# The second chunk's tokens fetched behind V's weights, c first, the last tile in two column steps, and another written-out order of all engines

## The chip, the cores and the metric

The kernel runs on one core of a Trainium2 chip. The metric is the device time of one execution in microseconds. The core has a matmul engine (PE, with its weight loads shown as PEld), VectorE (DVE), ScalarE (ACT), GpSimd (POOL) and SyncE (SP); SP here issues nearly all DMAs, in the order in which they stand on its queue. The clock that PE was granted is 1.00 throughout.

## What is computed

One transformer block over 2048 tokens of width 448, in bfloat16. Both halves are modulated by vectors that come from `silu(c) @ w_mod`.

```python
mod = (_silu(c) @ w_mod).reshape(c.shape[0], 6, 1, -1)
sa, ca, ga, sb, cb, gb = (mod[:, i] for i in range(6))
h = _layernorm(x) * (1 + ca) + sa
x = x + ga * attention(h, wqkv, wo)     # 16 heads of 28; each query sees 8 keys, 2 apart
h = _layernorm(x) * (1 + cb) + sb
x = x + gb * (silu(h @ w1) @ w2)        # hidden width 1792
```

## The kernel before

The tokens are cut into four chunks of 512 (`NC`), each of four tiles of 128 tokens; even and odd tokens are kept apart, since a query sees only keys of its own parity. For each chunk `norm1` normalizes the tokens (`Norm`: statistics on DVE by bn_stats, L497, or on ACT by two passes, L501 and L507; the power on POOL, L513; scaling, L523 to L527), turns them so that the width lies on partitions (chunk 0 on PE, L564; the others by DMA transposes on SP, L588) and applies the modulation (`on_pe`, L571 and L573; `on_dma`, L593 and L595). `project` multiplies with the weights of q and k (L668, copied out of PSUM at L672 by ACT or DVE) and of V (L688, copied out at L681). The q and k weights are first padded to 32 columns a head (`pad`, L603 and L605): four pads, for the four pieces of the width, k 0 to 3, and the matmuls (`phases`) take the pieces in the order 0, 3, 1, 2, two matmuls at a time.

Attention works on nine key blocks of 112 tokens a parity. `logits` (L716) multiplies keys and queries of all 16 heads into four PSUM banks, ACT takes the exponential (L724), DVE multiplies with a mask (L748); `values` multiplies with V and with a column of ones (L774), DVE divides by the sums (L779, L780), and a DMA transpose on SP (L784) puts the result into `oT`. `out_proj` (L804) multiplies with wo, and DVE adds the old x (L807). wo is multiplied with its gate on DVE (L916) as soon as the modulation rows (`mod_late`, L463 to L480) are there, and two DMAs (L917, L918) then copy parts of it to other partitions. `ffn1` normalizes again, multiplies with w1 (L831) and takes silu on ACT (L839); `ffn2` multiplies with w2 (L854), DVE adds x (L859), and SP stores the tile (L862). The last tile has a function of its own, `last_tile`: it works in two column halves, of which DVE adds one (L892) and ACT copies the other (L895; x was added by a matmul with the identity, L882), and one store (L898) follows.

w1 lies in four pieces: rows for k 0, 1 and 2 in `w1`, and the last 64 rows of each half of the columns in `w13` (L388), whose DMA has a source with an outermost dimension of two. `wqk3`, the last piece of the q and k weights, is cut in the same way. FFN1's matmuls take k 0 first and then k 3, from `w13`.

What sets the order: every piece of work is an operation of a `Plan` (`P.op`), with the operations that it needs and the PSUM banks that it takes. The planner could order them by estimated times, but for the fast path the order is written out: `ORDER` (L44) lists the numbers of all operations, with a letter where DVE or ACT is chosen and the banks behind a slash. `emit` issues them in this order, so each engine's program, and SP's and ACT's DMA queues, stand in it; each engine works through its own in order and waits for semaphores. Durations given in the operations serve the planner alone. The order is thus not changed by a changed duration, only by a changed `ORDER`.

A DMA uses one of eight semaphores in turn, so a DMA also waits until the eighth before it has landed. Before the change, ACT's queue issues the second half of chunk 0's tokens and then c. SP issues the first half, two pieces of w_mod, chunk 1's tokens, wqk3, V's weights in two DMAs, the q and k weights in two, the tokens of chunks 2 and 3, and then transposes and the other weights among each other: wo, the first part of w2 and w13 follow chunk 2's transposes, the three pieces of w1 stand between the transposes of `oT`.

Of the kernel before, what the change touches and what calls it, by code (L numbers as in the profile page):

```python
# [10 lines left out]
ALU = mybir.AluOpType  # L11
# [4 lines left out]
D = 448  # L16
# [221 lines left out]
def layer(ctx, tc, io, safe):  # L238
# [635 lines left out]

    def last_tile(k, j, u):

        box, n = {}, D // 2

        def part(o, f0, f1):
            if f0 == 0:  # L880
# [13 lines left out]
        def move(o):  # L894
            S.copy(out=box["o"][:, n:D], in_=box["ps"][1][:, 0:n])  # L895
# [128 lines left out]
```

## Time and profile before

| | |
|---|---|
| runs (median; lowest to highest) | 171.99 us; 170.29 to 173.71 us, 3 runs |
| profiled execution | 170.89 us, of which the span from first to last instruction is 169.2 us |
| PE busy | 160.8 us (95%) |
| ACT, DVE, POOL busy | 116.4, 99.1, 15.5 us |
| DMA | 17.48 MB moved |

In a row of the timeline stand the start, the length until the last of the merged instructions ends (both in us from the start of the span), the engine (SPq and ACTq are the issue of a DMA), line, operation, tile written <- tiles read, partitions x elements, and the count; in brackets, how long the engine stood idle before and what ended that. A DMA row of the issues gives the size and, where it is known, the time from issue to landing. In a row of stretches stand the stretch, its length, the busy time of each engine with its number of instructions, the granted clock, the share of 16 DMA engines that was busy, and GB/s.

### The profile page before, as it was taken

The page shows a single profiled execution, that of the slowest core. Times are in us where ns is not written, and L with a number is a line of the kernel's source. Part 1 is how long each engine was busy: PE and PEld are TensorE (multiplying, and loading weights), DVE is VectorE, ACT ScalarE, POOL GpSimd, SP SyncE. Part 2 cuts the span into 40 slices and gives each one's busy share as a digit, 9 for nine tenths or more (in the row PEclk, how much of TensorE's full clock was granted, in tenths as well). Part 3 has the DMA queues.
Part 4 walks back from the last instruction along what each step waited for, and adds up shares of the span by engine and source line. Part 5 has one row for each costly group of instructions (what it writes and reads, how often), then busy time and mean ns, then how long its engine had stood idle before and what let it go on. Part 6 is the DMA issues. An engine that isn't in the chain of part 4 may idle for free.

```text
span 169.2 us, 4278 instructions
## 1 busy us (share of the span) xinstructions
PE 160.8 (95%) x1763; PEld 79.9 (47%) x1764; DVE 99.1 (59%) x259; ACT 116.4 (69%) x166; POOL 15.5 (9%) x38
## 2 busy tenths in 40 slices
PE   7878999999999999999999999999999999999990
PEld 2344444353465554554464454564444454444670
DVE  2788899999988859475476309972950405100120
ACT  3676999899779967879996989484429903248000
POOL 4313112010000410011000000021001100000000
PEclk9999999999999999999999999999999999999999
DMA  5994999859994453500614001226410061100022
GB/s 180 251 324 171 190 303 164 265 154 101 142 248 109 112 103 76 169 0 9 119 27 111 2 0 31 54 63 117 113 54 6 0 124 38 49 0 0 27 62 68
DMA packets 32312, 17.48 MB, mean 103 GB/s; under 512 B 24157, under 2 KB 31453, under 8 KB 32285
## 3 DMA queue, kind: packets, MB, share of 16 engines
q1 hardware_dynamic: 32132, 16.90, 42.9%
q8 instruction: 16, 0.26, 0.7%
q10 hardware_dynamic: 152, 0.23, 0.4%
q14 instruction: 12, 0.09, 0.2%
HBM read 9.12 MB, written 1.84 MB: 65 GB/s over the span
## 4 chain that ended last, share of the span: by engine, by line
PE 74%; DMA 9%; DVE 7%; ACT 5%; issue 2%; SPq 0%
PE psum L831 25%; PE psum L854 24%; PE psum L804 7%; PE psum L668 6%; DMA wqk<-in_A_wqkv_dram 5%; PE psum L688 4%; PE psum L774 4%; PE psum L716 2%; DMA x_all<-in_A_x_dram 2%; DMA oT<-o 2%; DVE p L748 2%; PE psum L885 2%; ACT both L501 1%; ACT wp L603 1%; DVE wqk L595 1%
## 5 line engine op out<-in xcount | busy, mean ns | idle before, releaser
L831 PE MATMUL psum<-h,w 64*128 64x512 bf16 x392 | 43.7, 376 | 0.0
L854 PE MATMUL psum<-w,both 128*128 128x448 bf16 x210 | 42.1, 353 | 0.0
L839 ACT ACTIVATE both<-psum 128x1024 bf16<-128x1024 f32 x28 | 27.3, 1021 | 13.6 <-PE psum L831 13.6
L724 ACT ACTIVATE p<-psum 128x896 bf16<-128x896 f32 (+1 forms) x36 | 31.7, 935 | 5.0 <-PE psum L716 4.7
L831 PEld LDWEIGHTS <-w 64*128 64x128 bf16 x392 | 19.3, 94 | 22.2 <-issue 0.7
L854 PEld LDWEIGHTS <-both 128*128 128x128 bf16 x210 | 19.6, 98 | 19.1 <-issue 1.6
L513 POOL TENSOR_TENSOR rs<-rs,negh 128x2 f32<-128x2 f32 x16 | 12.5, 778 | 118.0 <-DVE rs L510 82.6
L748 DVE TENSOR_TENSOR p<-p,maskb 128x1792 bf16<-128x1792 bf16 (+1 forms) x18 | 19.5, 1099 | 4.8 <-ACT p L724 4.8
L859 DVE TENSOR_TENSOR ot<-psum,x_all 128x448 bf16<-128x448 f32 x15 | 9.2, 618 | 20.2 <-PE psum L854 15.9
L668 PE MATMUL psum<-h,wp 64*128 64x512 bf16 x168 | 19.8, 377 | 0.5 <-ACT wp L603 0.4
L668 PEld LDWEIGHTS <-wp 64*128 64x128 bf16 x224 | 10.4, 94 | 12.8 <-ACT wp L603 0.9
L507 ACT ACTIVATE mrow<-x_all,mv 128x448 bf16<-128x448 bf16 x16 | 10.7, 668 | 3.4 <-DVE mv L504 3.0
L804 PE MATMUL psum<-wo,oT 64*128 64x448 bf16 x112 | 12.7, 350 | 0.1
L593 ACT ACTIVATE h<-h,modc 128x512 bf16<-128x512 bf16 x7 | 5.5, 806 | 10.2 <-DMA h<-xn 10.2
L672 ACT CAST qk<-psum 128x1024 bf16<-128x1024 f32 x12 | 12.0, 1018 | 0.6 <-PE psum L668 0.6
L688 PE MATMUL psum<-wv,h 64*128 64x448 bf16 x98 | 11.3, 350 | 1.2 <-DMA wv<-in_A_wqkv_dram 1.1
L807 DVE SCALAR_TENSOR_TENSOR x_all<-psum,x_all 128x448 bf16<-128x448 f32 x16 | 9.5, 619 | 3.6 <-PE psum L804 3.6
L780 DVE TENSOR_TENSOR o<-psum,rc 112x448 bf16<-112x448 f32 (+1 forms) x18 | 11.2, 624 | 0.6
L779 DVE RECIPROCAL rc<-psum 112x16 f32<-112x16 f32 (+1 forms) x18 | 4.5, 251 | 10.2 <-PE psum L774 9.5
L774 PEld LDWEIGHTS <-p 128*128 128x128 bf16 x288 | 8.2, 96 | 3.3 <-issue 1.7
L774 PE MATMUL psum<-v,p 128*128 128x29 bf16 x288 | 9.0, 176 | 0.0
L595 DVE TENSOR_SCALAR h<-h,modc 128x512 bf16<-128x512 bf16 x17 | 6.1, 406 | 4.8 <-DMA h<-xn 4.6
(95 smaller groups left out, 144.6 us busy)
## 6 DMA issues: line engine op xcount, KB each, us to landing
out_dram<-ot SPq DMA_DIRECT2D x16, 112.0 KB, 1.8
both<-in_w_mod_dram SPq DMA_DIRECT2D x1, 1568.0 KB, 8.4
x_all<-in_A_x_dram SPq DMA_DIRECT2D x3, 448.0 KB, 8.1
w<-in_B_w_dram SPq DMA_DIRECT2D x3, 448.0 KB
w<-in_B_w_dram SPq DMA_DIRECT2D x1, 896.0 KB, 7.0
both<-in_w_mod_dram SPq DMA_DIRECT2D x2, 392.0 KB, 5.7
w<-in_B_w_dram SPq DMA_DIRECT2D x1, 672.0 KB, 5.4
wv<-in_A_wqkv_dram SPq DMA_DIRECT2D x2, 224.0 KB, 8.5
```

What stands on the lines that cost most here:

```text
L513: G.tensor_tensor(out=rs[:, j:j + n], in0=rs[:, j:j + n], in1=negh[:, 0:n], op=ALU.pow)
L668: return T.matmul(ps[:, j, :], lhsT=w.rearrange("p h d -> p (h d)"), rhs=h[rows, :, t, 128:128 + CP], start=start, stop=stop)
L672: copy_on(o)(out=qk[:, :, g, :, s0:s0 + CP], in_=ps.rearrange("p j (t s) -> p j t s", t=2))
L688: T.matmul(ps[:, par, 0:D], lhsT=h[rows, par, t, b0:b0 + 128], rhs=wv[rows, t, :], start=start, stop=stop)
L724: S.activation(out=out_, in_=ps[:, :, 0:4 * nq].rearrange("p j (g q) -> p j g q", q=nq), func=ACTF.Exp, scale=SCALE)
L748: V.tensor_tensor(out=p, in0=p, in1=maskb[:, 1 if b == 0 else 0, 0:nq].unsqueeze(1).to_broadcast([128, H, nq]), op=ALU.mult)
L774: T.matmul(ps[:, h, 0:DH + 1], lhsT=p[:, at:at + 128], rhs=v[:, h, 0:DH + 1], start=True, stop=True)
L780: V.tensor_tensor(out=box["o"][0:nq, off:off + D].rearrange("p (h d) -> p h d", d=DH), in0=ps[0:nq, :, 0:DH], in1=r.unsqueeze(2).to_broadc ...
L804: T.matmul(ps[par][:, 0:D], lhsT=oT[rows, t, par, s0:s0 + 128], rhs=wo[rows, par, t, :], start=start, stop=stop)
L831: return T.matmul(ps[:, j, :], lhsT=w, rhs=h[rows, :, t, :], start=start, stop=stop)
L839: silus[k].append(P.op(("act", 904.0), lambda o, i=i, box=box: S.activation(out=hid[:, k % 2, :, i, :], in_=box["ps"], func=ACTF.Silu), [m ...
L854: T.matmul(box["ps"][:, 0:D], lhsT=hid[:, k % 2, f % 2, f // 2, 128 * j:128 * j + 128], rhs=w2[:, f // 2 + 7 * (f % 2), :], start=(f == 0) ...
```

## The change

Four edits come together. First, c is loaded ahead of the tokens on ACT's queue. Second, the tokens of chunk 1 (448 KB) are made to depend on the issue of V's weights, and stand behind them on SP's queue, ahead of wqk3; those of chunks 2 and 3 come as one DMA of 896 KB in place of two. Third, the last tile is done in two column steps: its first 224 columns with all 14 matmuls, an add and a store of their own, ahead of two whole tiles; at the very end the other 224 columns in two pieces of 112, of which DVE adds one and ACT copies the other, and a second store. Fourth, `ORDER` is another, so that the order of the instructions on all engines differs, and with it which of ACT and DVE does a copy. Among what moves on SP's queue is w13: it now stands behind the two transposes of FFN chunk 0's input, as the last load ahead of FFN1; the first part of w2 stands ahead of wo; and the first transpose into `oT` stands ahead of the two copies of wo (L917 and L918; in the changed kernel lines from here on are some lines further down). The lag of 300 to 230 is an estimate for the planner.

```diff
@@ -42,29 +42,29 @@
 
 
 ORDER = (
-    "1 60/0 46 47 6 0 4 7 5 80 81 8 2 9 61 63 66 88 3 69 89 70/2 62 10 22 16 48 90 67 18 19 82 55 20 87 91 71 73/2 83 84 21 11 85v 74 97/3/4 86v 98 64 92 "
...
+    "1 44 45 46 47 0 4 5 52 7 8 78 9 58/0 2 59 6 3 67 68/2 69 60 62 79 80 71/2 10 11 51 86 87 88 63 65 85 89 20 18 72 22 23 56 81 90 16 82 57 83v 84v 92 "
...
 )
 
 
@@ -365,10 +365,10 @@
 
     def first_x(i):
         return dict(out=x_all[:, 2 * i:2 * i + 2, :].rearrange("p t d -> p (t d)"), in_=x_view[0, :, i, :])
-    act_q = [P.op(("none", 0.0), lambda o: nc.scalar.dma_start(**first_x(1)))]
-    act_q.append(P.op(("none", 0.0), lambda o: nc.scalar.dma_start(out=c4[:], in_=c.rearrange("o (k p) -> (o k) p", p=KM)), act_q[-1:]))
-    ld_c = [P.op(("none", 5200.0), lambda o: S.preload_act_table(ACTF.Silu), act_q[-1:])]
-    ld_x = [[load(224, **first_x(0)), P.op(("none", 4400.0), none, act_q[:1])]]
+    act_q = [P.op(("none", 0.0), lambda o: nc.scalar.dma_start(out=c4[:], in_=c.rearrange("o (k p) -> (o k) p", p=KM)))]
+    act_q.append(P.op(("none", 0.0), lambda o: nc.scalar.dma_start(**first_x(1)), act_q[-1:]))
+    ld_c = [P.op(("none", 3900.0), lambda o: S.preload_act_table(ACTF.Silu), act_q[-1:])]
+    ld_x = [[load(224, **first_x(0)), P.op(("none", 4800.0), none, act_q[-1:])]]
 
     def load_mod(k0, k1, c0, c1, after=()):
         return load((c1 - c0) * (k1 - k0) * KM / 512, wmod[0:KM, k0:k1, c0:c1], w_mod[KM * k0:KM * k1, c0:c1].rearrange("(k p) n -> p k n", p=KM), after)
@@ -380,7 +380,8 @@
     b = load(224, wqk[:, 1, :].rearrange("p (a n) -> p a n", a=2), dram(A_wqkv, 128, 0, ((1, 0, 128), (64, D, 2), (0, 1, D))), late)
     ld_qk = [[a], [b], [a], [load(112, wqk3[:], dram(A_wqkv, 128, D, ((128, -D, 2), (1, 0, K3), (0, 1, D))), late)]]
     ld_v = [load(224, wv[:, 2 * a:2 * a + 2, :], dram(A_wqkv, 192 * a, 2 * D, ((1, 0, 128), (128, 0, 2), (0, 1, D))), late) for a in range(2)]
-    ld_x += [[load(448, x_all[:, 4 * k:4 * k + 4, :].rearrange("p (i t) d -> p i (t d)", t=2), x_view[k], late)] * 2 for k in range(1, NC)]
+    ld_x.append([load(448, x_all[:, 4:8, :].rearrange("p (i t) d -> p i (t d)", t=2), x_view[1], [x["deps"][0] for x in ld_v])] * 2)
+    ld_x += [[load(896, x_all[:, 8:16, :].rearrange("p (k i t) d -> p k i (t d)", i=2, t=2), x_view[2:4].rearrange("c p i n -> p c i n"), late)] * 2] * 2
     ld_m2 = [load_mod(0, 4, 2 * D, 6 * D, late)]
     ld_o = [load(336, wo[:, 0, 0:3, :], rows3(A_wo), late), load(56, wo[half(0), 0, 3, :], A_wo[384:D, :], late)]
     ld_1 = [load(448, w1[:, k, :], B_w1[r:r + 128, :], late, rate=0.3) for k, r in ((0, 0), (2, 320))]
@@ -632,7 +633,7 @@
                 for part in range(2):
                     mm(box["ps"], part, kk, False, kk == 2, part)
         a = P.op(("pe", 4 * step), straight, deps, take=("one", "one") if split else ("big",), mode=1)
-        return box, a, P.op(("pe", 3 * step), crossed, [a], mode=1, lag=300.0)
+        return box, a, P.op(("pe", 3 * step), crossed, [a], mode=1, lag=230.0)
 
     qk_done, v_of, v_take, v_op, qk_mm, v_mm, halo = {}, {}, {}, {}, {}, {}, {}
     h1_done, h1_part = {}, {}
@@ -874,38 +875,43 @@
 
     def last_tile(k, j, u):
 
-        box, n = {}, D // 2
-
-        def part(o, f0, f1):
+        box, cut = {}, (0, D // 2, 3 * D // 4, D)
+
+        def part(o, f0, f1, i0, i1):
             if f0 == 0:
-                box["ps"] = [onet(), onet()]
-                T.matmul(box["ps"][1][:, 0:n], lhsT=ident[:], rhs=x_all[:, u, n:D], start=True, stop=False)
+                box.setdefault("ps", []).extend(onet() for _ in range(i0, i1))
+                if i1 == 3:
+                    T.matmul(box["ps"][2][:, 0:cut[3] - cut[2]], lhsT=ident[:], rhs=x_all[:, u, cut[2]:cut[3]], start=True, stop=False)
             for f in range(f0, f1):
-                for i in range(2):
-                    T.matmul(box["ps"][i][:, 0:n], lhsT=hid[:, k % 2, f % 2, f // 2, 128 * j:128 * j + 128], rhs=w2[:, f // 2 + 7 * (f % 2), n * i:n * i + n],
-                             start=(f + i == 0), stop=(f == NF - 1))
+                for i in range(i0, i1):
+                    T.matmul(box["ps"][i][:, 0:cut[i + 1] - cut[i]], lhsT=hid[:, k % 2, f % 2, f // 2, 128 * j:128 * j + 128], rhs=w2[:, f // 2 + 7 * (f % 2), cut[i]:cut[i + 1]],
+                             start=(f == 0 and i < 2), stop=(f == NF - 1))
 
         def hold(o):
             box["o"] = outb[o["slot"]["out"]]
 
-        def add(o):
-            V.tensor_tensor(out=box["o"][:, 0:n], in0=box["ps"][0][:, 0:n], in1=x_all[:, u, 0:n], op=ALU.add)
+        def add(o, i):
+            V.tensor_tensor(out=box["o"][:, cut[i]:cut[i + 1]], in0=box["ps"][i][:, 0:cut[i + 1] - cut[i]], in1=x_all[:, u, cut[i]:cut[i + 1]], op=ALU.add)
 
         def move(o):
-            S.copy(out=box["o"][:, n:D], in_=box["ps"][1][:, 0:n])
-
-        def store(o):
-            nc.sync.dma_start(out=out_view[u // 4, u // 2 % 2, u % 2], in_=box["o"][:])
-        prev = None
-        for f0, f1 in ((0, 4), (4, 8), (8, 12), (12, 14)):
-            need = silus[k][f0 // 2:f1 // 2] + w2_gated + ([x1_done[u]] if f0 == 0 else [])
-            prev = P.op(("pe", 194.0 * (f1 - f0) + (98.0 if f0 == 0 else 0.0)), lambda o, f0=f0, f1=f1: part(o, f0, f1), need + [prev], take=("one", "one") if f0 == 0 else ())
-            if f0 == 0:
-                first = prev
-        ot = P.op(("none", 0.0), hold, [first], take=("out",))
-        ad = P.op(("dve", 310.0), add, [prev, ot], give=((first, "one"),))
-        mv = P.op(("act", 242.0), move, [prev, ot], give=((first, "one"),))
-        sp(550.0, store, [ad, mv], 1200.0, ((ot, "out"),), (390.0, 500.0, 360.0))
+            S.copy(out=box["o"][:, cut[2]:cut[3]], in_=box["ps"][2][:, 0:cut[3] - cut[2]])
+
+        def store(o, i, n):
+            nc.sync.dma_start(out=out_view[u // 4, u // 2 % 2, u % 2][:, cut[i]:cut[n]], in_=box["o"][:, cut[i]:cut[n]])
+        prev, done = None, []
+        for i0, i1 in ((0, 1), (1, 3)):
+            for f0, f1 in ((0, 8), (8, 14)):
+                need = silus[k][f0 // 2:f1 // 2] + w2_gated + ([x1_done[u]] if f0 == 0 else [])
+                prev = P.op(("pe", 97.0 * (f1 - f0) + (50.0 if i0 and not f0 else 0.0)), lambda o, a=(f0, f1, i0, i1): part(o, *a), need + [prev], take=("one",) * (i1 - i0) if f0 == 0 else ())
+                if f0 == 0:
+                    first = prev
+            if i0 == 0:
+                ot = P.op(("none", 0.0), hold, [first], take=("out",))
+                done = [P.op(("dve", 310.0), lambda o: add(o, 0), [prev, ot], give=((first, "one"),))]
+                sp(550.0, lambda o: store(o, 0, 1), done, dma=(390.0, 500.0, 250.0))
+            else:
+                ad = [P.op(("dve", 195.0), lambda o: add(o, 1), [prev, ot], give=((first, "one"),)), P.op(("act", 150.0), move, [prev, ot], give=((first, "one"),))]
+                sp(550.0, lambda o: store(o, 1, 3), ad, 1200.0, ((ot, "out"),), (390.0, 500.0, 250.0))
 
 
     for k in range(NC):
```

44 rows, old and new, of the table ORDER are left out of this document.

## The prediction, made before the changed kernel was run

> **What bounds the kernel now.** I read the busy shares and slices first, then a table of stretches, then the timeline of each stretch, then the DMA issues.
>
> ```profile
> PE 160.8 (95%) x1763; PEld 79.9 (47%) x1764; DVE 99.1 (59%) x259; ACT 116.4 (69%) x166; POOL 15.5 (9%) x38
> PE   7878999999999999999999999999999999999990
> PE 74%; DMA 9%; DVE 7%; ACT 5%; issue 2%; SPq 0%
> ```
> ```profile
> 16.00:44.00 28.00, 27.50 (x382) 12.33 (x380) 26.90 (x59) 26.79 (x42) 3.23 (x7) 1.00 0.85 194
> 44.00:66.00 22.00, 22.00 (x336) 11.83 (x334) 17.42 (x46) 17.86 (x26) 2.62 (x2) 1.00 0.67 126
> 66.00:122.00 56.00, 56.00 (x634) 28.46 (x630) 33.53 (x81) 43.87 (x58) 2.76 (x4) 1.00 0.28 64
> 122.00:165.00 43.00, 43.00 (x325) 21.67 (x324) 10.17 (x30) 18.04 (x25) 1.38 (x2) 1.00 0.14 35
> ```
> The columns of the second fence are the stretch, its length, then busy time of PE, PEld, DVE, ACT, POOL, the granted clock, DMA share and GB/s. From 44 to 165 us PE is never idle, so nothing can be won there, and whatever makes PE wait there is paid in full. From 16 to 44 us PE, DVE and ACT are all near full; PE idles 0.50 us. Before 16 us the start waits for loads. The change keeps PE's work, so a gain has to come from the start or from the tail.
>
> **The start (V's weights ahead of the second chunk's tokens, c first).**
>
> ```profile
> 12.16 3.27 PE L688 MATMUL psum<-wv,h 64*128 64x448 bf16 x28 [1.05 <-DMA wv<-in_A_wqkv_dram]
> 14.03 1.78 ACT L603 COPY wp<-wqk 128x896 bf16<-128x896 bf16 x2 [1.29 <-DMA wqk<-in_A_wqkv_dram]
> 14.73 0.39 DVE L603 COPY wp<-wqk 128x896 bf16<-128x896 bf16 x1 [0.79 <-DMA wqk<-in_A_wqkv_dram]
> 15.80 2.72 SPq L588 DMA_TRANSPOSE h<-xn  x2
> 15.86 7.97 PE L668 MATMUL psum<-h,wp 64*128 64x512 bf16 x70 [0.43 <-ACT wp L603]
> 21.43 0.80 ACT L593 ACTIVATE h<-h,modc 128x512 bf16<-128x512 bf16 x1
> 22.14 1.90 ACT L672 CAST qk<-psum 128x1024 bf16<-128x1024 f32 x2
> 23.76 0.73 PE L716 MATMUL psum<-qk 28*128 28x128 bf16 x16
> ```
> V's matmuls waited 1.05 us for wv; with wv ahead of 560 KB (x of chunk 1 and wqk3) this wait goes. What is late next is wqk: the bytes ahead of it on SP's queue are the same set in another order, so it lands at 14.03 again. The pads now are k 0 and 1 on ACT and k 2 and 3 on DVE (before: 2 and 0 on ACT, 1 and 3 on DVE), so the first q/k matmul (k 0) can start after one ACT pad, at 14.03+0.89=14.9 instead of 15.86. But its third pair needs pad k 1 at 15.8, and the next bound is ACT: from 14.03 to chunk 1's h at 21.43 it runs the same ten instructions in both orders (two pads, two V copies, four sums, two squares). Chunk 1's h therefore comes at 21.4 to 22.2 again, PE waits there instead, and the early start is given back: 0. Chunk 1's tokens land later by V's 448 KB, some 1.2 us at the 378 GB/s of the row of 13 us below. DVE's statistics of them move behind it; the old order held DVE until 14.73 for a pad, so its transposes, at 15.80 before, move by about 0.2 us, under ACT's chain. Moving c saves nothing: the modulation weights decide the first h. One DMA for chunks 2 and 3 carries the same bytes, and their first reader (ACT's sums) stands behind the V copies: 0.
>
> **The order from 22 to 44 us.** The first logits wait for three q/k copies; the new order has these three on ACT behind h (22.14+3x0.95=25.0) where the old one shared them with DVE. So L716, at 23.76 before, moves by 1.2 us, and PE does 8 more L668 matmuls meanwhile (0.86 us): +0.35. Further on:
>
> ```profile
> 29.31 0.94 PE L463 MATMUL psum<-both,screp 112*32 112x448 bf16 x16
> 33.99 1.08 DVE L916 TENSOR_TENSOR wo<-wo,gbc 128x1792 bf16<-128x1792 bf16 x1
> 35.10 0.54 SPq L917 DMA_DIRECT2D wo<-wo  x1
> 41.94 1.39 PE L804 MATMUL psum<-wo,oT 64*128 64x448 bf16 x8
> ```
> ```profile
> wo<-wo SPq DMA_DIRECT2D x1, 168.0 KB, 5.7
> ```
> ```profile
> 39.34 3.02 DMA oT<-o
> 54.64 0.76 PE psum L804 x8
> ```
> The last fence is from the chain of work that ended last: start, length, what. The modulation rows (L463) move behind 56 matmuls of L668, 28 of L688, three L716 and one L774, where 42, 14, two and none preceded them from chunk 1's start. That is some 3.5 us, so the wo gate on DVE (35.07 before) ends near 38 and the two shifted copies of wo start 3 us later. SP now issues the first oT transpose ahead of them, the second behind. The first L804 took 1.39 us where eight such matmuls take 0.76, a wait of 0.6 that ends with oT (39.34+3.02=42.36). I followed the new queues of PE, ACT and DVE with these durations up to it: it ends near 44.2 (before: 43.3) with 8 more L668 matmuls done (0.86). Sum of the stage: 0. Bounds: the gain can be no more than PE's 0.50 idle, the 0.6 and the two start waits (1.05+0.43), 2.6 us in all; the loss is some 1.5 us if the wo copies take 5.7 us again behind a gate at 38 and PE waits for them.
>
> **The step that decides: w13 on SP's queue.** The last piece of B_w1 (w13, 224 KB, L388) stood in row 28.50 below as the second DMA. In the new order it stands behind both transposes of FFN chunk 0's h and is the last load ahead of FFN1.
>
> ```profile
> w<-in_B_w_dram SPq DMA_DIRECT2D x1, 224.0 KB
> ```
> ```profile
> 13.00:14.00 1.00, 1.00 (x14) 0.62 (x12) 0.91 (x5) 0.00 (x0) 0.71 (x2) 1.00 1.06 378
> 35.20:36.00 0.80, 0.80 (x11) 0.26 (x8) 0.80 (x4) 0.80 (x2) 0.24 (x1) 1.00 0.14 52
> ```
> ```profile
> 28.50 2.34 SPq L362 DMA_DIRECT2D w<-in_B_w_dram  x2
> 58.66 3.98 SPq L588 DMA_TRANSPOSE h<-xn  x2
> 64.54 0.81 ACT L593 ACTIVATE h<-h,modc 128x512 bf16<-128x512 bf16 x1 [1.74 <-DMA h<-xn]
> 64.61 1.05 DVE L595 TENSOR_SCALAR h<-h,modc 128x512 bf16<-128x512 bf16 x3
> 65.16 0.73 PE L804 MATMUL psum<-wo,oT 64*128 64x448 bf16 x6
> 65.73 3.40 PE L831 MATMUL psum<-h,w 64*128 64x512 bf16 x30
> ```
> ```profile
> x_all<-in_A_x_dram SPq DMA_DIRECT2D x1, 224.0 KB, 3.3
> ```
> At 35.2 us w13 alone is under way: DMA share 0.14, that is 2 of 16 engines, and 52 GB/s, against 378 GB/s with all engines. Its source has an outermost dimension of two, so two engines carry it. Its 229 KB need 229/52=4.4 us on the wire. In the old order it was issued by 30.84 and FFN1 began at 65.73, so all of this was hidden. Now: SP was free after the second h transpose at 62.64. PE's work ahead of the first L831 is the same in both orders, but the out projection that feeds this transpose stands ahead of one L716 and two L774 now (0.31+0.8 us), so I take 61.9 for w13's issue. The first two x loads of the same size, issued together, took 3.3 us to land, of which 458 KB at 378 GB/s are 1.2 us of data; so I take 2.1 us for lead and completion. It lands at 61.9+2.1+4.4=68.4; without the earlier transpose at 69.1. PE reaches the first FFN1 matmul at 65.7, does the pair of k 0 (0.2), and the next pair is k 3, which reads w13: it waits from 65.95 to 68.4 or 69.1. I take the first, 2.4 us. Everything else of PE stands behind it in order. Bounds: 0.5 (PE itself a microsecond late, w13 issued earlier still) and 3.5.
>
> The Trainium skill, page "DMA: Bandwidth & Descriptors", section "Why a DMA increments its semaphore by 16 and not by 1", has the number of engines as the largest number up to 16 that divides the slowest dimension, and so two here, as the share of 0.14 has it. By that page's 27 GiB/s for an engine ("Specifications") the data would take an estimated 4.0 us and the stall would be 0.4 us shorter than mine; the measured 52 GB/s decides.
>
> **The last tile.**
>
> ```profile
> 62.28 0.96 PE L774 MATMUL psum<-v,p 128*128 128x29 bf16 x32
> ...
> 164.25 0.62 DVE L859 TENSOR_TENSOR ot<-psum,x_all 128x448 bf16<-128x448 f32 x1 [2.29 <-DMA out_dram<-ot]
> 165.10 0.39 DVE L892 TENSOR_TENSOR ot<-psum,x_all 128x224 bf16<-128x224 f32 x1 [0.23 <-PE psum L885]
> 165.14 0.35 ACT L895 CAST ot<-psum 128x224 bf16<-128x224 f32 x1 [9.00 <-PE psum L885]
> 165.55 0.33 SPq L898 DMA_DIRECT2D out_dram<-ot  x1
> ```
> 14 of the 28 matmuls of 224 columns become 28 of 112: the same columns, and 32 matmuls of 29 columns, each with a weight load of its own, in 0.96 us (row 62.28) show that weight loads keep up. The last add goes from 0.39 to about 0.27 us (0.62 for 448 columns, 0.39 for 224). The three last whole tiles now share one output buffer: tile 13's add waits for tile 12's store, as the 2.29 us above do now, and the first half's add stands behind it on DVE. Gain 0.1, bounds -0.3 and +0.5; the last store's landing stays.
>
> **Sum.** 170.89 (profiled execution, span 169.2) + 0 (start) + 0 (22 to 44 us) + 2.4 (w13) - 0.1 (tail) = 173.2. The median of the runs is 171.99, 1.1 above the profiled execution, which would make 174.3; I predict 173.8, between the two, and add the same 0.6 to the profiled basis in each rival.
>
> **Rivals.** First: w13 arrives in time: 170.89-0.1+0.6=171.4, to 171.9 with a rest of the stall. For it speaks that PE or h could be late themselves; against it that w13's issue and h hang on the same transpose: h needs its landing and a modulation (64.54+0.81-62.64=2.7 us after SP is free), w13 needs 2.1+4.4=6.5. It decides when PE comes to FFN1 after 68. Second, faster: PE's start gain is kept because chunk 1's h comes earlier, the stage to 44 us loses its waits, and w13 is none. At most 2.6+0.1, so 168.8 to 170.5; it needs ACT's chain to be shorter than its 7.4 us, and the new order has none of its instructions gone. Third, slower still: the wo copies behind the late gate hold PE at the first L804 by 1.5 us, and w13 by 2.4: 170.89+3.9-0.1+0.6=175.3; it decides when the gate ends after 38. Fourth, PE's clock:
>
> ```profile
> 1.26 4.88 PE L416 MATMUL psum<-both 128*128 128x512 bf16 x11 [1.26 <-DVE both L313]
> 6.92 1.04 PE L416 MATMUL psum<-both 128*128 128x512 bf16 x4
> ```
> The first matmuls took 4.88/11=0.44 us each, later ones 0.26. If the wait at 66 us returned PE to that pace for 4.88 us, this would cost 4.88x(1-0.26/0.44)=2.0 us more: 175.8. The wait of 1.05 us before V left no such slow matmuls. The Trainium skill, page "TensorE: Matmul & The Clock Gate", Part 1, halves the clock after an idle window of about 3.4 us; no wait in this trace is that long.
>
> **How the numbers follow.** w13's stall as computed 0.57, w13 in time 0.20, faster 0.08, wo and w13 0.10, clock 0.05. The likeliest's own range is 171.5 to 175.5 (stall 0.5 to 3.5, basis up to 0.6 either way). The range 170.2 to 176.2 leaves out the lower part of the faster case and the tail of the last two. Two per cent (3.4 us, about what a measurement of this kernel tells from no change) is 168.55 below and 175.43 above: above lie the last two cases and the upper edge of the first, 0.20; below only the second rival's far end with the scatter of the runs, 0.04; within 0.76.
>
> **What would show it.** After: V without a wait for wv near 11 us; the first L669 near 15; chunk 1's h still at 21.4 to 22.2; and in the waits of PE one L832 of about 2.4 us near 66 us that ends with the DMA of B_w. Wrong would be: no PE gap near 66 us, w13 on 16 engines, or a PE gap of a microsecond between 22 and 44.

## The result and the profile after

| | before | after |
|---|---|---|
| median of the runs | 171.25 us (170.29 to 173.71, 6 runs) | 178.24 us (176.91 to 178.56, 6 runs) |
| profiled execution, span | 169.2 us | 176.4 us |
| mean granted clock of it | 1.00 | 0.984 |

The changed kernel is slower: ratio 1.041, 95% interval 1.035 to 1.046, or 7 us. The forecast was 173.8 us with a range of 170.2 to 176.2; the time lies 2.0 us above the range.

The page of the changed kernel, PE's busy slices and the granted clock (a slice is 4.4 us):

```profile
PE   7987999999989992999999999999999999999990
PEclk9999999999999999699999999999999999999997
PE 66%; DMA 12%; ACT 7%; DVE 6%; issue 2%; SPq 2%; POOL 2%; ACTq 0%; DVEq 0%
```

PE has one hole, in the slice from 66 us on, and the next slice has a granted clock of 0.6. Before, neither was there. In the chain of work that ended last, PE has 66% and DMA 12%, where PE had 74% and DMA 9%.

The same stretches in numbers (columns as in the prediction's table):

```profile
16.00:44.00 28.00, 26.86 (x362) 12.38 (x359) 24.32 (x57) 27.00 (x42) 4.85 (x5) 1.00 0.80 193
44.00:66.00 22.00, 21.16 (x336) 11.48 (x337) 19.24 (x47) 17.59 (x26) 1.69 (x2) 1.00 0.57 113
66.00:71.00 5.00, 1.23 (x14) 0.44 (x12) 3.44 (x9) 3.51 (x6) 0.00 (x0) 1.00 1.40 81
71.00:76.00 5.00, 5.00 (x34) 1.95 (x32) 0.00 (x0) 1.33 (x2) 0.00 (x0) 0.66 0.50 142
76.00:127.00 51.00, 51.00 (x583) 26.56 (x581) 31.82 (x76) 35.36 (x45) 2.85 (x4) 1.00 0.25 54
```

From 44 to 66 us PE idles 0.84 us where it never idled before; from 66 to 71 it works 1.23 us out of 5; from 71 to 76 it is busy throughout, at a clock of 0.66. From 76 us on it is never idle again up to its last matmul, which ends at 171.9 us, ahead of the last slice with its clock of 0.7. Cut finer, the stretch shows that 0.6 and 0.66 are means of two values:

```profile
71.72:75.12 3.40, 3.40 (x18) 1.23 (x16) 0.00 (x0) 0.55 (x1) 0.00 (x0) 0.50 0.49 149
75.13:78.50 3.37, 3.37 (x36) 1.64 (x34) 0.09 (x1) 1.77 (x3) 0.00 (x0) 1.00 0.02 5
```

For 3.4 us the clock stands at half, and then it is full again. PE's timeline says what each of these is (start, length, what, and in brackets the idle time before it and what ended that):

```profile
10.75 3.30 PE L689 MATMUL psum<-wv,h 64*128 64x448 bf16 x28
14.70 0.60 PE L669 MATMUL psum<-h,wp 64*128 64x512 bf16 x4 [0.65 <-ACT wp L604]
...
21.66 3.00 PE L669 MATMUL psum<-h,wp 64*128 64x512 bf16 x22 [0.33 <-DVE h L596]
24.84 0.40 PE L717 MATMUL psum<-qk 28*128 28x128 bf16 x16 [0.18 <-ACT qk L673]
...
44.29 0.38 PE L717 MATMUL psum<-qk 28*128 28x112 bf16 x16 [0.42 <-DVE qk L673]
51.20 1.04 PE L669 MATMUL psum<-h,wp 64*128 64x512 bf16 x8 [0.55 <-ACT v L682]
...
66.72 0.38 PE L832 MATMUL psum<-h,w 64*128 64x512 bf16 x2
70.87 4.88 PE L832 MATMUL psum<-h,w 64*128 64x512 bf16 x28 [3.77 <-DMA w<-in_B_w_dram]
75.59 0.92 PE L805 MATMUL psum<-wo,oT 64*128 64x448 bf16 x8
```

FFN1 (L832 here, L831 before) does its first pair at 66.72 and then waits 3.77 us for w13. SP's timeline and the chain of work show the load that it waits for:

```profile
61.30 1.54 SPq L589 DMA_TRANSPOSE h<-xn  x1
62.90 0.61 SPq L362 DMA_DIRECT2D w<-in_B_w_dram  x1
64.82 2.52 SPq L785 DMA_TRANSPOSE oT<-o  x2
```
```profile
62.90 7.92 DMA w<-in_B_w_dram
```

The load is issued at 62.90 and lands 7.92 us later. Two stretches of that time (last two columns: DMA share, GB/s):

```profile
64.50:65.00 0.50, 0.50 (x10) 0.26 (x6) 0.47 (x3) 0.22 (x1) 0.00 (x0) 1.00 0.00 0
68.00:70.00 2.00, 0.00 (x0) 0.00 (x0) 1.86 (x5) 1.51 (x4) 0.00 (x0) 1.00 0.13 50
```

From 64.5 to 65.0 us, 1.6 us after the issue, nothing moves; from 68 to 70 us 0.13 of 16 engines, that is two, move 50 GB/s.

With these lines the 7.2 us between the two spans can be laid out along PE's work. FFN1 starts at 66.72 where it started at 65.73: 1.0. The wait: 3.8. Its first 30 matmuls took 3.40 us before, so 28 of them 3.40x28/30 = 3.2; they take 4.88 now: 1.7. That makes 6.5 by 75.6 us; the remaining 0.7 lies behind that. The last add is at 171.92, where it was at 165.10, so 0.3 came up to there and 0.4 after it:

```profile
171.92 0.28 DVE L894 TENSOR_TENSOR ot<-psum,x_all 128x112 bf16<-128x112 f32 x1 [0.45 <-PE psum L887]
```

SP's two last issues, the stores of the first half and of the second:

```profile
171.62 0.38 SPq L900 DMA_DIRECT2D out_dram<-ot  x1
...
172.26 1.55 SPq L900 DMA_DIRECT2D out_dram<-ot  x1
```

Before, the last store's issue took 0.33 us (165.55).

### The profile page after: what moved, and what is told of

Its sections match the earlier page's. It is cut to its first block, busy times and chain, and to the rows that moved or that the text cites. A ratio compares the mean times of both kernels' runs of the same rounds, so it can differ in the third digit from the quotient of the medians.

```text
span 176.4 us, 4308 instructions
## 1 busy us (share of the span) xinstructions
PE 163.4 (93%) x1778; PEld 81.0 (46%) x1778; DVE 100.3 (57%) x261; ACT 115.5 (65%) x164; POOL 16.8 (10%) x38
## 4 chain that ended last, share of the span: by engine, by line
PE 66%; DMA 12%; ACT 7%; DVE 6%; issue 2%; SPq 2%; POOL 2%; ACTq 0%; DVEq 0%
PE psum L832 25%; PE psum L855 23%; DMA wqk<-in_A_wqkv_dram 5%; PE psum L805 5%; DMA w<-in_B_w_dram 4%; PE psum L669 4%; PE psum L717 3%; PE psum L689 2%; DMA h<-xn 2%; PE psum L775 2%; POOL rs L514 2%; SPq L362 2%; ACT qk L673 2%; PE psum L887 2%; ACT both L502 1%
## 5 line engine op out<-in xcount | busy, mean ns | idle before, releaser
L832 PE MATMUL psum<-h,w 64*128 64x512 bf16 x392 | 45.7, 387 | 3.8 <-DMA w<-in_B_w_dram 3.8
L832 PEld LDWEIGHTS <-w 64*128 64x128 bf16 x392 | 20.1, 96 | 26.9 <-DMA w<-in_B_w_dram 4.2
L514 POOL TENSOR_TENSOR rs<-rs,negh 128x2 f32<-128x2 f32 x16 | 13.7, 859 | 125.3 <-DVE rs L511 125.3
L669 PE MATMUL psum<-h,wp 64*128 64x512 bf16 x168 | 20.9, 377 | 1.8 <-ACT wp L604 0.9
L673 ACT CAST qk<-psum 128x1024 bf16<-128x1024 f32 x13 | 12.9, 1019 | 1.0 <-PE psum L669 1.0
L805 PE MATMUL psum<-wo,oT 64*128 64x448 bf16 x112 | 12.8, 350 | 0.0
L594 ACT ACTIVATE h<-h,modc 128x512 bf16<-128x512 bf16 x6 | 4.8, 808 | 11.0 <-DMA h<-xn 11.0
L511 DVE TENSOR_SCALAR rs<-mv 128x2 f32<-128x2 f32 x16 | 2.6, 163 | 12.6 <-ACT mrow L508 12.5
L775 PE MATMUL psum<-v,p 128*128 128x29 bf16 x288 | 9.5, 176 | 0.0
```

The source lines that it names most:

```text
L514: G.tensor_tensor(out=rs[:, j:j + n], in0=rs[:, j:j + n], in1=negh[:, 0:n], op=ALU.pow)
L669: return T.matmul(ps[:, j, :], lhsT=w.rearrange("p h d -> p (h d)"), rhs=h[rows, :, t, 128:128 + CP], start=start, stop=stop)
L673: copy_on(o)(out=qk[:, :, g, :, s0:s0 + CP], in_=ps.rearrange("p j (t s) -> p j t s", t=2))
L775: T.matmul(ps[:, h, 0:DH + 1], lhsT=p[:, at:at + 128], rhs=v[:, h, 0:DH + 1], start=True, stop=True)
L805: T.matmul(ps[par][:, 0:D], lhsT=oT[rows, t, par, s0:s0 + 128], rhs=wo[rows, par, t, :], start=start, stop=stop)
L832: return T.matmul(ps[:, j, :], lhsT=w, rhs=h[rows, :, t, :], start=start, stop=stop)
```

## The experiments

Theory A: w13 stands too late on a queue that gives it two engines, PE waits for it, the wait lowers PE's clock, and that is nearly all of the loss. Rival B: the new order costs the time as a whole, and w13's wait merely covers other waits. A number by which a kernel "gains" is taken against 178.24, which was measured at another time than the runs; ratios are against the kernel before on the same chip, beside the run, where its median was 171.1 to 171.8 us. Each load has a second number in `ORDER`, for its landing, which issues nothing and moves with it; the cuts show it in run 2 alone.

**1. w13 early (changed kernel).** Only the load's token (its number in `ORDER`) moves, to the place that it had among the weight loads.

```diff
-... 230 231 34 279/6 280 ... 350 366 38 359/0 ...
+... 230 231 34 38 279/6 280 ... 350 366 359/0 ...
```

> The changed kernel, with one load moved: w13 (224 KB of B_w1) is issued among the other weight loads of the middle stage, ahead of the second transpose of chunk 0's h, as the kernel before does it. Nothing else differs. Theory A (w13 on two engines, issued too late, and TensorE's clock after the wait, are nearly all of the loss): the wait of 3.8 us at the first L832 goes, the 28 matmuls behind it take 3.2 us and not 4.9, and the time falls from 178.2 by 5.5 to 6 us to 172.2 to 172.8, about 1 us above the kernel before. Rival B (the new order as a whole costs the time, and w13's wait only covers other waits, that of h above all): the wait at FFN1 stays in part under another name, and the time stays at 175 or more. If the start of the new order were worth something after all, the time would fall below 171.

Measured: 174.09 us, ratio 1.015 (1.009 to 1.021). The clock stays full and FFN1 has no wait, a gain of 4.2 us. But 2.6 us of loss are left, more than theory A's 1: FFN1 begins only at 68.50, since PE now waits at an out projection (L804 here).

```profile
55.71 1.04 PE L804 MATMUL psum<-wo,oT 64*128 64x448 bf16 x8 [1.67 <-DMA oT<-o]
68.50 3.40 PE L831 MATMUL psum<-h,w 64*128 64x512 bf16 x30
```

Both theories hold in part: A has the larger share, but B has one.

**2. w13 late (kernel before).** The converse: the load's token behind both transposes of FFN chunk 0's h, all else as before.

```diff
-... 42 234v 43 40 210v ... 368 396 397 395 ...
+... 42 234v 43 210v ... 368 396 40 397 41 395 ...
```

> The kernel before, with w13's load alone moved behind both transposes of FFN chunk 0's h. Theory A: PE waits at the first FFN1 group (65.73 us before). SP is free after the second transpose at 62.64; a landing 8.0 us after the issue, as in the changed kernel (62.90 to 70.87), puts the end of the wait at 70.6: 4.6 us of wait, and 1.8 us more for the slow clock behind it, so 171.3 + 6.4 = 177.5 to 178. Rival B: with the old order around it the wait is mostly covered, 172 to 174. Rival C (the wait costs, but the clock does not fall in this order): 175.5 to 176.

Measured: 177.94 us, ratio 1.038 (1.031 to 1.044). This one token makes the kernel before as slow as the changed kernel.

```profile
PEclk9999999999999998599999999999999999999997
```
```profile
65.42 0.38 PE L830 MATMUL psum<-h,w 64*128 64x512 bf16 x2
71.16 5.58 PE L830 MATMUL psum<-h,w 64*128 64x512 bf16 x28 [5.36 <-DMA w<-in_B_w_dram]
```

(L830 here.) PE comes to FFN1 1.3 us earlier than in the changed kernel, so it waits longer, 5.36 us, and the 28 matmuls take 5.58. Rivals B and C both fall: in the old order nothing covers the wait, and the clock drops there too.

**3. w13 in two DMAs (changed kernel).** Place unchanged; two DMAs of 64 rows each.

```diff
-ld_1.append(load(224, w13[:], dram(B_w1, 128, F // 2, ((128, -F // 2, 2), (1, 0, K3), (0, 1, F // 2))), late, rate=0.3))
+def two(o):
+    for a, (r, c0) in enumerate(((128, F // 2), (256, 0))):
+        nc.sync.dma_start(out=w13[half(a), :], in_=B_w1[r:r + K3, c0:c0 + F // 2])
+ld_1.append(sp(max(400.0, 224 / 0.31), two, [begin] + late, 500.0, dma=(600.0, 1300.0, 150.0 + 224 / 0.3))[0])
```

> The changed kernel, with w13's load left at its place but cut into two transfers of 64 rows each, whose outermost dimension is 64 and not two. Theory A (two engines at 52 GB/s carry it): with 16 engines the 224 KB need 0.6 to 1.2 us on the wire in place of 4.4, so w13 lands some 3.2 to 3.8 us earlier, at 67.1 to 67.7; the wait falls to 0.2 to 0.9 us, the clock stays, and the time is 172.4 to 173.8. Rival D (not the wire but the queue delays it: the issue at 62.90 itself, lead and completion, or the transposes ahead of it): the wait stays at 3 us or more and the time at 177 or more.

Measured: 174.03 us, ratio 1.018 (1.010 to 1.026).

```profile
w<-in_B_w_dram SPq DMA_DIRECT2D x2, 112.0 KB, 2.7
```
```profile
66.61 3.52 PE L835 MATMUL psum<-h,w 64*128 64x512 bf16 x30
```

The two halves land 2.7 us after their issue instead of 7.9 and FFN1 has no wait, at the same place in the queue: rival D falls. The rule in the Trainium skill, page "DMA: Bandwidth & Descriptors", section "Why a DMA increments its semaphore by 16 and not by 1" (the largest number up to 16 that divides the slowest dimension), gives 16 engines for 64 rows and two for the old source. The traces agree: 0.13 of 16 engines for the old source, and for the halves a landing after 2.7 us, though their engines were not counted.

**4, 5 and 9. The wait filled with matmuls (changed kernel).** 17 matmuls of 512 columns on landed data, into a PSUM tile that the group behind them starts anew. Runs 4 and 5 differ from 9 in the group alone: `(k, i)` was (0, 0) and (0, 1), and the one that stands first in PE's order is (0, 4).

```diff
+            for _ in range(fill):
+                T.matmul(box["ps"][:, 0, :], lhsT=ident[:], rhs=w1[:, 0, 0:512], start=True, stop=True)
             for kk in (0, 3, 1, 2):
...
-            box, first, m = phases(mm(i), 512, nrm.done + ld_1)
+            box, first, m = phases(mm(i), 512, nrm.done + ld_1, fill=17 if (k, i) == (0, 4) else 0)
```

> The changed kernel, with 17 matmuls of 512 columns put ahead of the first FFN1 group, on data that landed long before, into a PSUM tile that the group then starts anew (their result is overwritten). They need 17 x 0.213 = 3.6 us at full clock and lie inside the wait of 3.8 us. Theory A (the clock falls because PE is idle for 3.8 us): the granted clock stays full, the 28 matmuls behind the wait take 3.2 us and not 4.9, and the time falls by 1.5 to 2 us to 176.2 to 176.8, though the wait for w13 still ends at 70.9. Rival E (the slow matmuls are slow for another reason, such as operands or transfers at that place): they stay at 4.9 us and the time at 178 or above.

> The changed kernel with the 17 filling matmuls of 512 columns ahead of the FFN1 group that comes first in PE's order (in the run before they had been put ahead of a group that comes ten microseconds later). They lie inside the wait for w13, 66.7 to 70.9. Theory A (PE's idle time of 3.8 us lowers the clock): no slice of the granted clock below 9, the 28 matmuls behind the wait take 3.2 to 3.4 us and not 4.9, time 178.2 - 1.7 = 176.2 to 176.8, with the wait for w13 still ending at 70.9. Rival E (they are slow for another reason): 4.9 us again, and the time at 178 or above.

> The changed kernel with the 17 filling matmuls now at their place, ahead of the FFN1 group that stands first in PE's order (the two runs before had them behind it, at 81 us). They run while w13 is awaited. Theory A (PE's idle time of 3.8 us lowers the clock): no slice of the granted clock below 9, the 28 matmuls behind the wait take 3.2 to 3.4 us and not 4.9, the wait for w13 still ends at 70.9 to 71.1, and the time is 178.2 - 1.7 = 176.2 to 176.8. Rival E (they are slow for another reason than idle time): 4.9 us again and the time at 178 or above.

Measured: run 4 183.4 us (1.066, 1.055 to 1.077), run 5 183.07 us (1.067, 1.061 to 1.073), run 9 176.32 us (1.029, 1.023 to 1.034). Runs 4 and 5 missed their purpose: the matmuls came behind the wait and only made the kernel longer, as the first fence shows. Run 4 tells only that 17 of them are 3.84 us, and, in the second fence, that the matmuls behind a wait of 4.14 us are slow again.

```profile
81.95 3.84 PE L622 MATMUL psum<-w,ident 128*128 128x512 bf16 x17
```
```profile
71.22 5.80 PE L834 MATMUL psum<-h,w 64*128 64x512 bf16 x28 [4.14 <-DMA w<-in_B_w_dram]
```

Run 9 has them in the wait:

```profile
PEclk9999999999999999999999999999999999999999
```
```profile
67.74 3.84 PE L622 MATMUL psum<-w,ident 128*128 128x512 bf16 x17
71.51 3.41 PE L834 MATMUL psum<-h,w 64*128 64x512 bf16 x30
```

Here the granted clock stays full, 30 matmuls take 3.41 us as in the kernel before, and the time is 1.9 us lower (2.1 by the two ratios), although w13 lands no earlier. So the slow matmuls come from PE's idle time and rival E falls. What a drop costs hangs on how long the clock stays down. First run 2, then run 4:

```profile
69.20:76.00 6.80, 4.84 (x24) 1.82 (x26) 1.14 (x2) 0.35 (x1) 0.00 (x0) 0.50 0.47 126
69.72:76.53 6.81, 5.31 (x26) 1.90 (x28) 0.15 (x1) 2.38 (x4) 0.00 (x0) 0.50 0.45 123
```

In these two the clock stood at half for 6.8 us, and PE worked 4.84 and 5.31 us of them; in the changed kernel it was 3.4 us, all of them worked. Half of each is 2.4, 2.7 and 1.7 us, and by 2.4, 2.6 and 1.7 us the 28 matmuls were longer than 3.2 (5.58, 5.80 and 4.88). So the loss doesn't follow the order of the waits, which were 5.36, 4.14 and 3.77 us.

The Trainium skill, page "TensorE: Matmul & The Clock Gate", Part 1, has the clock halved after an idle window of about 3.4 us, with windows that run free of the kernel's start. The traces agree in part: the stretches at half clock are one or two times 3.4 us long, they come with the waits of 3.77, 4.14 and 5.36 us, and the wait of 1.67 us (run 1) left the clock at 1.00. But in the changed kernel PE still worked 0.83 of the 3.40 us ahead of the drop (68.30 to 71.70), and in the profiled execution of run 7, below, the clock fell at the kernel's start with no such wait:

```profile
5.60:9.00 3.40, 2.39 (x41) 1.49 (x40) 2.08 (x11) 1.70 (x5) 2.15 (x9) 1.00 1.08 303
9.02:12.42 3.40, 3.40 (x24) 2.00 (x22) 2.19 (x7) 2.74 (x6) 0.12 (x1) 0.50 1.08 319
```

Ahead of that drop PE worked 2.39 of 3.40 us, and its longest wait there was 0.74 us. In the kernel before it worked 2.16 of the 3.40 us from 9.00 to 12.40, and the clock stayed full. What brings the drop in run 7 is not found. The clock of 1.00 in the kernel before, too, is that of its profiled execution: of its 23 runs beside runs 9 to 12, six had a mean clock of 0.989 or 0.990, which is what one such stretch would make, and took 171.9 to 173.2 us; the others had 0.995 or more and a median of 170.7.

**6. One last store (kernel of run 3).** The last tile's row is stored once, behind both column steps.

```diff
-                sp(550.0, lambda o: store(o, 0, 1), done, dma=(390.0, 500.0, 250.0))
+                sp(550.0, none, done, dma=(390.0, 500.0, 250.0))
...
-                sp(550.0, lambda o: store(o, 1, 3), ad, 1200.0, ((ot, "out"),), (390.0, 500.0, 250.0))
+                sp(550.0, lambda o: store(o, 0, 3), ad, 1200.0, ((ot, "out"),), (390.0, 500.0, 250.0))
```

> The kernel with w13 in two DMAs, and the last tile's row stored by one DMA behind both of its column steps, in place of one DMA for each step. In the kernel with two stores SP took 0.38 us to issue the first half's and 1.51 us to issue the second, where a store takes 0.33 us elsewhere, so that SP ended 1.2 us later than it would. Theory T (the second store's issue is held up by the stores right ahead of it): with one store the last issue takes 0.3 to 0.4 us and the time falls by 0.8 to 1.2 us, from 174.0 to 172.8 to 173.2. Rival U (the last store is slow wherever it stands, or the end of the program waits for something else): 173.7 or more.

Measured: 174.13 us, ratio 1.017 (1.013 to 1.021), against 174.03 for run 3: by the runs no difference. In the profile the last issue does take 0.33 us, at 167.03, and the span is 171.2 in place of 171.8; but runs of this order scatter by 2 us (172.71 to 174.74) for a reason that run 10 looks for. The issue is shown, its worth in time is not, by this run.

**7. The start of the change alone (kernel before).** V's loads ahead of the second chunk's tokens, k 0's pad first on ACT. c stays behind the tokens, and the tokens of chunks 2 and 3 stay two DMAs.

```diff
-... 10 22 16 48 90 67 18 19 82 55 20 ... 13 78a 68 79v 76a ...
+... 10 18 20 22 16 48 90 67 19 82 55 ... 13 76a 68 79v 78a ...
```

> The kernel before with the start of the change alone: V's two loads ahead of the second chunk's tokens, and the first of ACT's two pads is that of k 0. All the rest of the order is the old one. The prediction's step (the early start is given back, since ACT's chain sets chunk 1's h): V's matmuls lose their wait of 1.05 us, the first q/k matmul comes at 14.7 to 15.0, chunk 1's h at 21.2 to 22.2 as before, PE waits for it, and the time is that of before within 0.4 us. Rival S (the start is worth something in itself, and the new order behind it loses it): 0.7 to 1.3 us faster than before. Rival R (the later tokens delay chunk 1's h): 0.5 us or more slower.

Measured: 171.37 us, ratio 1.002 (0.999 to 1.004): no difference. The wait for wv is gone, q/k starts 0.7 us earlier, and PE loses it again at chunk 1's h. (V itself starts no earlier here, at 12.35 where it was 12.16, since this execution has the half clock from 9.02 to 12.42 us. The other 11 runs have a mean clock of 0.995 or more and took 170.9 to 172.2 us.)

```profile
12.35 3.02 PE L687 MATMUL psum<-wv,h 64*128 64x448 bf16 x28
15.18 6.22 PE L667 MATMUL psum<-h,wp 64*128 64x512 bf16 x56
21.95 2.03 PE L667 MATMUL psum<-h,wp 64*128 64x512 bf16 x14 [0.55 <-DVE h L594]
23.91 0.63 PE L715 MATMUL psum<-qk 28*128 28x128 bf16 x16
```

The first logits come at 23.91, where they came at 23.76. Rivals S and R fall; the prediction's step holds as far as this run has it, without c.

**8 and 12. Chunk 1's h ahead of work for later chunks.** Run 8 is run 6's kernel, run 12 is run 7's.

```diff
 run 8
-... 70 183 235 191 193 192 182 110 184 185 234 108v ... 194 161a ...
+... 70 183 235 191 193 192 110 108v ... 194 161a 234 182 184 185 ...
 run 12, beside run 7's
-... 119a 77v 114/0 147v 105/1 26 148v ... 195 194 196 109 110v 115 164a ...
+... 119a 147v 148v 77v 114/0 105/1 26 ... 109 110v 115 164a 195 194 196 ...
```

> The kernel with w13 in two DMAs and one last store, and chunk 1's h modulated ahead of work for later chunks: one sum of ACT's (0.77 us) and one pair of DVE statistics (0.8 us) move behind it. In the changed kernel h's second transpose had landed at 19.9 while ACT came to h at 21.26 and DVE at 20.56. If ACT's and DVE's order, and not the transfer, holds h: h ends at 20.9 to 21.1 on both, PE's wait of 0.33 us for it goes, and the time is 0.3 to 0.5 us below that of the kernel with one last store. If the lead of 0.75 us that PE has there is lost further on anyhow (v and q/k copies of 44 to 51 us): no difference.

> An attempt at a version that beats both kernels: the kernel before with V's loads ahead of the second chunk's tokens and k 0's pad first (0.2% from before in its run), and now with what chunk 1's h waits for moved up: DVE makes the first two xn tiles ahead of its second pad, and two of ACT's sums for later chunks (0.77 us each) stand behind h. In the run without these moves PE waited 0.55 us for h, whose transpose landed at 21.1 by DVE's wait. If that wait was all that ate the early start: 0.4 to 0.7 us faster than before (170.4 to 170.8). If the copies of q and k, which follow h on ACT and DVE, are next: no difference within 0.3 us.

Measured: run 8 173.75 us, ratio 1.014 (1.009 to 1.019); run 12 171.03 us, ratio 0.998 (0.995 to 1.002). PE's wait for chunk 1's h is gone in both, and waits for other copies stand in its place. In run 8:

```profile
15.96 8.41 PE L671 MATMUL psum<-h,wp 64*128 64x512 bf16 x74 [0.23 <-ACT wp L606]
25.10 0.40 PE L719 MATMUL psum<-qk 28*128 28x128 bf16 x16 [0.73 <-ACT qk L675]
```

Where the changed kernel waits 0.33 us for h and then 0.18 for a q/k copy, this one waits 0.73 for the copy. Its median is 0.4 us below run 6's, which would fit the first of the two expectations, but the two intervals overlap, so neither is shown. In run 12 PE waits 0.41 and 0.2 us for copies of q and k instead. Run 12 was to beat both kernels; it can't be told from the kernel before, and no other run is faster.

**10. The load behind the fourth oT transpose (kernel of run 6).** The load of k 1 (448 KB) moves among the early weights.

```diff
-... 231 34 279/6 ... 380 381 36 355/2/1 ...
+... 231 34 36 279/6 ... 380 381 355/2/1 ...
```

> The kernel with w13 in two DMAs and one last store, and the load of k 1 of B_w1 (448 KB) issued some 23 us earlier, with the other weights, so that it no longer stands right behind the fourth oT transpose at 52 us. In two of the profiled executions of kernels of this order PE waited 1.5 to 1.7 us for that transpose at 55.7: the last piece of it landed at 55.6, behind that load's first data, where it landed at 53.1 in the others. Theory L (the load delays the transpose's last piece): no wait of over 0.3 us at the L804 of 54 to 56 us, and the time falls from 174.1 by 0.8 to 1.5 us. Rival M (the wait comes from the transposes' own issue, 1.3 us longer in those executions): the wait stays in some executions and the time within 0.4 us of 174.1.

Measured: 173.62 us, ratio 1.014 (1.010 to 1.019), 0.5 us below run 6, with intervals that overlap. The wait at the out projection is still there, at 55.19, now with ACT's v copy put down as what ended it:

```profile
55.19 1.04 PE L807 MATMUL psum<-wo,oT 64*128 64x448 bf16 x8 [1.35 <-ACT v L684]
```

Theory L falls. What goes with the wait is the row of M, SP's issue of one transpose of h at 44 to 45 us. First run 10, then run 6, whose profiled execution had no such wait:

```profile
44.66 2.44 SPq L591 DMA_TRANSPOSE h<-xn  x1
47.15 5.18 SPq L787 DMA_TRANSPOSE oT<-o  x4
```
```profile
44.87 1.23 SPq L592 DMA_TRANSPOSE h<-xn  x1
46.15 5.76 SPq L788 DMA_TRANSPOSE oT<-o  x4
```

In runs 1, 5, 8, 9 and 10 this issue took 2.1 to 2.5 us and PE waited 1.35 to 1.67 us at 55 us; in the changed kernel and in runs 3, 4 and 6 it took 1.23 us and there was no such wait. That is all that is shown; what makes the issue long in some executions wasn't found.

**11. The last tile of the change alone (kernel before).** The new last tile's function, and its tokens at the places of the old one's.

```diff
-... 751/2/3 729 ... 661 755 662 752 733 734 735 753 754 757 756 758 759 704 ...
+... 751/2 729 ... 661 662 752 733 734 735 757/3/1 753 754 755 756 758 760 759 761 762 704 ...
```

> The kernel before with the last tile of the change alone: two column steps, two stores, three accumulators. The prediction had -0.1 us for it (bounds -0.3 to +0.5). Theory T (the last store's issue takes 1.5 us right behind the store of the first half, and nothing is won in the arithmetic): 0.6 to 1.1 us slower than before. If the prediction's -0.1 holds: the same within 0.3 us.

Measured: 172.09 us, ratio 1.005 (1.002 to 1.009), that is 0.9 us slower (0.3 to 1.5). Its last add ends at 165.96 and SP has 0.99 us of issue left:

```profile
165.68 0.28 DVE L893 TENSOR_TENSOR ot<-psum,x_all 128x112 bf16<-128x112 f32 x1 [0.46 <-PE psum L886]
```
```profile
166.02 0.99 SPq L899 DMA_DIRECT2D out_dram<-ot  x1
```

The add is shorter by 0.1 us, as forecast, the last issue is longer by 0.7 us. Theory T holds for the time; the issue itself took 0.99 us and not 1.5.

## Why the prediction was wrong

- **The start (0): right.** V without a wait at 10.75, first q/k at 14.70 (forecast 14.9), ACT's h from 21.26 (forecast 21.4 to 22.2), first logits 1.1 us later (forecast 1.2). Run 7 has the start without the move of c at +0.3 us (0.2%), which is not clear of zero. c by itself was not tried.
- **22 to 44 us (0): right for what it looked at.** The late wo gate was no wait: the two copies of wo were issued at 37.62 and 38.18, and the first out projection (L805) ran 42.95 to 43.87 without one. That rival (0.10) did not happen.
- **"PE's work ahead of the first L831 is the same in both orders": wrong by 1.0 us.** The queues had been followed to the first out projection, at 44 us, and from there to 66 us the old time was kept. The new order has two waits of PE in that stretch, 0.42 and 0.55 us, for copies of q/k and v. Runs 1, 3, 6, 8 and 10, all without the wait for w13, stay 2.4 to 3.1 us slower than before by their ratios (1.4 to 1.8% of 171.5). In the profiles of runs 1 and 3 some 0.9 of that is the last tile (runs 6, 8 and 10 store its row once), about 1 in all five is these waits, and the rest the wait at 55 us that some executions have. This split is read from profiles, and no run tries it. Which of the many moved instructions brings these about was not tried.
- **w13's stall (2.4): mechanism right, term mis-sized.** The wait came where it was put, for the cause given, and measured 3.77 us. The issue was set at 61.9 and came at 62.90, as the second transpose of h went out at 61.30; lead and data were set at 6.5 us and took 7.92. The pace was right, 50 GB/s from 68 to 70 us where 52 were assumed, so most of the 1.4 us more is time in which the load moved slower or not at all, as from 64.5 to 65.0 us. Two oT transposes go onto the same queue behind it; whether they hold it up was not tried. With 1.0 us for the issue, these 1.4, and 1.0 off for PE's own lateness, the 2.4 become 3.8. In run 2, where PE was on time, the wait was 5.36.
- **The clock (rival with 0.05): the step that failed, together with the size of the stall.** The sum has it at nothing. It was set aside since no wait of the trace before was 3.4 us long, with the stall's own upper bound at 3.5 us: the step took the middle of its range and asked there whether the clock falls. The wait became 3.77 us and the clock fell to half for 3.4 us, 1.7 us by the matmuls; run 9 puts it at 1.9 us. That rival's price of 2.0 is close partly by luck: it reckoned 4.88 us at the slow pace of the kernel's first matmuls, where it was half the clock for 3.4 us. That no wait is 3.4 us long was no safeguard either, as the start of run 7 shows. Stall and clock are not independent chances: a stall a little longer than expected brings the second price with it, so the upper end belonged at 177.5, which is 175.5, the stalled case's own upper end, and 2.0 more. Even that is 0.7 us short of 178.24. (That case's lower end comes out at 171.3 by its own terms, and not 171.5.)
- **The last tile (-0.1): wrong in sign.** 0.9 us in run 11 (0.3 to 1.5), beyond the bound of +0.5. The arithmetic was right (0.28 us for the last add); the second store's issue was costed at nothing, while the row of SP's issues had to be asked what two stores right behind one another cost.

The sum in the changed kernel's own terms: 1.0 (to 66 us) + 3.8 (w13) + 1.7 (clock) + 0.7 (last tile and end) = 7.2. The prediction's sum has 2.3 in its place (2.4 for w13 less 0.1 for the last tile), so 4.9 us are missing: 1.7 for the clock, 1.4 for the stall, 1.0 for PE's lateness and 0.8 for the last tile. The clock is the largest, but none of them alone carries 173.8 out of the range. In the runs, the wait and the clock together are worth 4.1 to 4.2 us (runs 1 and 3 against the changed kernel), less than their 5.5 us in the profile. Part of the difference is rival B's share, waits that w13's wait covered and that come to light without it: 1.67 us at 55 us and 0.15 at 110 in run 1, 0.43 us for oT at 109 us in run 3. Whether that is all of it is not shown.

## What to carry to other kernels

A load is put on a queue by when its data must be there, less its whole time from issue to landing, and that time hangs on how many engines its outermost dimension lets it use: cut into 64 rows, the same bytes at the same place took 2.7 us and not 7.9. A wait of PE of 3.8 us and more brought a second price with it in every trace here, 1.7 to 2.6 us: keep it well below, or fill it with matmuls that cost nothing there, and give a forecast both prices together. When an order of all engines is replaced, follow the queues to the end of the stage that the argument needs, and count the issue of every added DMA on the path to the end.

## What the runs showed of the hardware that was not expected

- With waits of 3.77 to 5.36 us the granted clock fell to 0.50 for 3.4 or 6.8 us, and 28 matmuls took 4.88 to 5.80 us in place of 3.2: half of what PE worked at half clock was lost. A wait of 1.67 us left it at 1.00.
- The clock also fell with no wait over 0.74 us ahead of it: from 9.02 to 12.42 us in the profiled execution of run 7, after 3.40 us of which PE worked 2.39.
- A store issued right behind the store of the other half of the same row took SP 0.99 to 1.55 us to issue, in place of 0.33.
- The same DMA transpose took 1.23 us to issue in some executions and 2.1 to 2.5 in others, and PE's wait of 1.35 to 1.67 us ten microseconds later went with it.
